# Strassen once more inside two of seven products: the second layer of a fused convolution and feed-forward kernel laid out by column tiles

## The chip, the cores and the metric

The kernel runs on one core of one Trainium2 chip. The metric is device time in microseconds (us) of that core. The profile comes from one execution recorded by the hardware profiler. Engines: TensorE (PE) multiplies, VectorE (DVE) and ScalarE (ACT) work elementwise on SBUF and PSUM, GpSimd (POOL) works elementwise on SBUF, SyncE (SP) issues most DMAs. Each runs its own queue in order, and semaphores make one wait for another.

## The reference

`x` is 8 x 4096 x 192, i.e. 32768 tokens of 192 features. A causal depthwise convolution of 7 taps (softmax of a weight per head) is followed by a feed-forward block with 2048 hidden units:

```python
out = np.einsum('hk,bskhg->bshg', w, x_unf)      # 7 taps, w = softmax(weight)
h = x @ w_in                                     # 192 -> 2048
g = h * np.clip(h + 3.0, 0.0, 6.0) / 6.0         # hard swish
return (g @ w_out).astype(np.float32)            # 2048 -> 192
```

All is fp32. The input arrives transposed, features ahead of tokens.

## The kernel before

**Rounds.** The tokens are cut into 32 blocks of 1024, each of two halves of 512 (index k). Round 0 is special (weights are still being loaded and prepared; `out_direct`, L364, does its second layer plainly). Rounds 1 to 31 (L775) are alike: `first_layer(i)` (L478), then `second_layer(i)` (L532). The schedule is written out by hand (`tc.manual_schedule`): the order of the calls in the source is each engine's order.

**First layer.** For each of 8 chunks c of hidden units and 2 groups (own and swapped halves) PE makes three accumulating passes (HIGH, LOW, MIX: the fp32 numbers are split into parts for the faster fp32r format) with row tiles of 64. ACT scales PSUM by 4097 between them (L501), then ACT (`relu`, L301) and DVE (`gate`, L305) make the activations `g`. Between groups DVE works through `jobs`: the taps of the next block's convolution (L729), and what is left over of the round before. [...]

**Second layer.** `g` is seen as a 2 x 2 block matrix A (token half by hidden half, each 8 chunks of 128), `w_out` as a 2 x 2 block matrix B (hidden half by output half of 96 columns). The product is done in the Strassen-Winograd form with seven products instead of eight:

```
S1 = A21+A22  S2 = S1-A11  S3 = A11-A21  S4 = A12-S2
T1 = B12-B11  T2 = B22-T1  T3 = B22-B12  T4 = T2-B21
P1 = A11 B11  P2 = A12 B21  P3 = S4 B22  P4 = A22 T4
P5 = S1 T1    P6 = S2 T2    P7 = S3 T3
```

Each product is 96 output columns, i.e. three thirds of 32 (index q, `QS` = 32), by 512 tokens, by 8 chunks. A matmul (`mm`, L336) has 32 columns and runs in one of four column tiles of PE (`tile_position`); `side_by_side` (L349) issues four streams in turn, so that four matmuls run together: a quartet. `three` (L420) puts a product's three thirds and a third of another into the four tiles, `four` (L413) any four parts, `by_quarters` (L423) cuts one third's chunks into four. Each quartet of streams fills one PSUM bank; ACT copies pieces out to SBUF (L437, L540), and DVE adds them up with the other banks (`add`, L445), transposes 32 x 32 blocks (`store`, L447) and hands the rows to SP to store. S3 is made by GpSimd (L401) pair by pair during the first layer, S1 by an accumulating DMA from GpSimd's queue (L528) but for the last pair, which DVE adds; S2 (into A11's place) and S4 (into A12's) by DVE (`g_sums`, L391) in the second layer. After the first layer `halves_of_y` (L751) splits the next block's convolution result and swaps its halves by DMA. `finish` (L566) is left for the next first layer, in the last round it is done in two halves of 256 tokens.

Of the kernel before, what the change touches and what calls it, by code (L numbers as in the profile page):

```python
# [8 lines left out]
ALU = mybir.AluOpType  # L9
# [16 lines left out]
def kernel(  # L26
# [34 lines left out]
    cst = ctx.enter_context(tc.tile_pool(name="cst", bufs=1))  # L61
    xs = ctx.enter_context(tc.tile_pool(name="xs", bufs=1))
    ys = ctx.enter_context(tc.tile_pool(name="ys", bufs=1))
    ot = ctx.enter_context(tc.tile_pool(name="ot", bufs=3))
    ps = ctx.enter_context(tc.tile_pool(name="ps", bufs=1, space=bass.MemoryType.PSUM))
    start_pools, first_in = ExitStack(), ExitStack()
    stg = start_pools.enter_context(tc.tile_pool(name="stg", bufs=8))
# [49 lines left out]
    w_out = cst.tile([P, NP, 7, DH], F32, name="w_out")  # L117
    B11, B12, B21, B22, T1, T2, T4 = range(7)
    T3 = B12

    w_in_bits = moe_w_in.bitcast(U32).rearrange("(p s) (c f w) -> c p s f w", s=K3, f=P, w=2)
    w_out_bits = moe_w_out.bitcast(U32).rearrange("(k c p) w -> p c k w", p=P, k=2)
# [230 lines left out]

    every = range(NP)

    def store_rows(i, k, q, xt, j, dma=nc.sync, tokens=slice(0, N)):

        t0 = i * TB + k * N
        dma.dma_start(
            out=out[t0 + tokens.start : t0 + tokens.stop, q * QS : (q + 1) * QS].rearrange("(t r) d -> r t d", r=QS),  # L360
            in_=xt[j * QS : (j + 1) * QS, tokens].rearrange("r (t d) -> r t d", d=QS),
        )

    def out_direct(i, work):  # L364

        parts = [(k, q) for k in range(G) for q in range(G * NQ)]
        for r in range(0, len(parts), 4):
            b = take()
            bank = psum[:, b]
            streams = []  # L370
            for j, (k, q) in enumerate(parts[r : r + 4]):
                streams.append([
                    m
                    for mms in zip(*(
                        mm(bank, j, dff_half(h * G + k), h * 2 + q // NQ, q % NQ, every,
                           h == 0, h == 1)
                        for h in range(2)
                    ))
                    for m in mms
                ])  # L380
            side_by_side(*streams)
            if r == 0:
                for u in work:
                    u()
            xt = ot.tile([P, N], F32, name="xt")
            nc.vector.transpose(out=xt[:], in_=bank)
            give(b)
            for j, (k, q) in enumerate(parts[r : r + 4]):
                store_rows(i, k, q, xt, j)

    def g_sums(engine, which, slots, width):  # L391

        forms = {
            3: (S3, A11, A21, ALU.subtract),
            2: (S2, S1, A11, ALU.subtract), 4: (S4, A12, S2, ALU.subtract),
        }
        for n in which:
            o, a, b, op = forms[n]
            for p in slots[::width]:
                r = slice(p, p + width)  # L400
                engine.tensor_tensor(out=o[:, r], in0=a[:, r], in1=b[:, r], op=op)  # L401


    prod = {
        1: (A11, B11), 2: (A12, B21), 3: (S4, B22), 4: (A22, T4),
        5: (S1, T1), 6: (S2, T2), 7: (None, T3),
    }

# [37 lines left out]

    def store(i, c, k, half_, qs=range(NQ), queues=(nc.sync,), tokens=slice(0, N)):  # L447

        xt = ot.tile([P, N], F32, name="xt")
        r = slice(qs[0] * QS, (qs[-1] + 1) * QS)  # L450
        nc.vector.transpose(out=xt[r, tokens], in_=c[r, tokens])  # L451
        for q in qs:
# [6 lines left out]
    def r32(ap):  # L459
        return ap.bitcast(F32R)  # L460
# [13 lines left out]
        nc.scalar.mul(r32(mix), mix, -4096.0)  # L474

    free_slots = list(range(4))

    def first_layer(i, jobs):  # L478

# [5 lines left out]
        def mms(n, part, start=False, stop=False):  # L485
            group, c = divmod(n, NP)
            for s in range(K3):
                for k in range(2):
                    r = slice(k * D2, (k + 1) * D2)
                    nc.tensor.matmul(  # L490
                        out=psum[:, 2 * slots[n] + k], lhsT=r32(w_in_parts[part][r, c, s]),
                        rhs=r32(y_parts[part][r, group, s]),
                        start=start and s == 0, stop=stop and s == K3 - 1,
                        skip_group_check=True,
                    )
# [20 lines left out]
        for n in range(count):  # L516
# [4 lines left out]
                begin(n + 2)  # L521
            for job in jobs.get(n, ()):
                job()
            if n > NP and n % 2:
                pair = slice(n - NP - 1, n - NP + 1)
                g_sums(nc.gpsimd, (3,), range(NP)[pair], 2)
                if n + 1 < count:
                    nc.gpsimd.dma_start(out=S1[:, pair], in_=A22[:, pair], accum_op=ALU.add)  # L528
                else:
                    add(S1[:, pair], A21[:, pair], A22[:, pair])  # L530

    def second_layer(i, between):  # L532
        last = i + 1 == NB
        ours = [free_slots.pop(0) for _ in range(3 + last)]
        free_banks[:] = [2 * n + k for n in ours for k in range(2)]
        both = nc.sync, nc.scalar
        p1, p2, p4, u2, u3 = (cs.tile([DH, N], F32, name=f"c{k}") for k in range(5))
        two, third = rows_of(0, 2), rows_of(2, 3)
        b, bank = three(1, 2, 0)
        nc.scalar.copy(out=p1[:], in_=bank[m])  # L540
        piece(p2, 0, bank, NQ)
        b, bank = four((2, 1), (2, 2), (4, 0), (4, 1))
        for dst, q, j in ((p2, 1, 0), (p2, 2, 1), (p4, 0, 2), (p4, 1, 3)):
            piece(dst, q, bank, j)
        g_sums(nc.vector, (2,), every, 4)
        add(p2[:], p1[:], p2[:])
        store(i, p2, 0, 0)
        p5 = cs.tile([DH, N], F32, name="c1")
        b7, bank7 = three(7, 4, 2)
        piece(p4, 2, bank7, NQ)  # L550
        g_sums(nc.vector, (4,), every, 4)
        b, bank = three(6, 5, 0)
        piece(p5, 0, bank, NQ)
        add(u2[:], p1[:], bank[m])
        add(u3[:], u2[:], bank7[m])
        add(p4[:], u3[:], p4[:], ALU.subtract)
        store(i, p4, 1, 0)
        for job in between:
            job()
        b, bank = by_quarters(5, 1)  # L560
        pieces(p5, 1, bank)
        add(u2[two], u2[two], p5[two])
        add(p5[two], u3[two], p5[two])
        store(i, p5, 1, 1, range(2))

        def finish(bank, **part):  # L566
            t = part.get("tokens", slice(0, N))
            add(u2[:, t], u2[:, t], bank[m, t])
            add(u2[third, t], u2[third, t], bank[rows(NQ), t])
            store(i, u2, 0, 1, **part)  # L570
            add(u3[third, t], u3[third, t], bank[rows(NQ), t])
            store(i, u3, 1, 1, range(2, 3), **part)

        if last:
            for t in range(0, N, N // 2):
                bank = psum[:, take()]
                ts = slice(t, t + N // 2)
                side_by_side(*[
                    product(bank, j, n, q, tokens=ts)
                    for j, (n, q) in enumerate([(3, 0), (3, 1), (3, 2), (5, 2)])  # L580
                ])
                finish(bank, queues=both, tokens=ts)
            return []
        b, bank = three(3, 5, 2)
        free_slots.extend(ours)
        return [lambda: finish(bank)]

    def rows_of(q0, q1):
        return slice(q0 * QS, q1 * QS)
# [18 lines left out]
    with tc.manual_schedule():  # L608
# [106 lines left out]
        while n < len(units):  # L715
# [1 line left out]
            clamp(n + 1)  # L717
            split(n + 2)
            n += 1
        w_sums(((T1, B12, B11), (T2, B22, T1), (T4, T2, B21)))  # L720
        start_pools.close()
        late = ctx.enter_context(tc.tile_pool(name="late", bufs=1, reuse_waits="tile"))
        w_in_parts = [late.tile([P, NP, K3, P], F32, name=f"w_in{n}") for n in range(3)]
# [8 lines left out]
                ))  # L732
            return jobs

        y_parts = []

        def y_high():
            high_of(y_parts[HIGH][:, 0], y[:])
            swap(y_parts[HIGH][:, 1], y_parts[HIGH][:, 0])

        def y_low():
            nc.vector.tensor_tensor(  # L742
                out=r32(y_parts[LOW][:, 0]), in0=y[:], in1=y_parts[HIGH][:, 0], op=ALU.subtract
            )
            swap(y_parts[LOW][:, 1], y_parts[LOW][:, 0])

        def y_mix():
            from_high(y_parts[MIX][:, 0], y_parts[HIGH][:, 0], 1.0 + EPS, y[:], ALU.subtract)
            swap(y_parts[MIX][:, 1], y_parts[MIX][:, 0])

        def halves_of_y():  # L751
            y_high()
            y_low()
            y_mix()

        def prepare():
            for n in range(0, NP, 4):
# [3 lines left out]
                job()  # L761
            first_in.close()
            later = ctx.enter_context(tc.tile_pool(name="later", bufs=1, reuse_waits="tile"))
            y_parts.extend(later.tile([P, 2, K3, N], F32, name=f"y{n}") for n in range(3))
            halves_of_y()
            x_tiles[2] = load_x(2, nc.gpsimd)

        out_direct(0, [prepare])
        w_sums(((T3, B22, B12),))
        last = ctx.enter_context(tc.tile_pool(name="last", bufs=1, reuse_waits="tile"))  # L770
        S3 = last.tile([P, NP, N], F32, name="s3")[:]
        cs = ctx.enter_context(tc.tile_pool(name="cs", bufs=1, reuse_waits="tile"))
        conv = conv_jobs(2)
        left = []
        for i in range(1, NB):  # L775
            jobs = {2 * n + 1: [job] for n, job in enumerate(conv[1:])}
            jobs[-1] = left
            if i == 1:
                jobs = {n + 2: job for n, job in jobs.items()}
                jobs[1] = conv[:1]  # L780
            first_layer(i, jobs)
            if i + 1 < NB:
                halves_of_y()
            if i + 2 < NB:
                x_tiles[i + 2] = load_x(i + 2)
            conv = conv_jobs(i + 2) if i + 2 < NB else []
            left = second_layer(i, conv[:1])


# [31 lines left out]
```

## Time and profile before

2251.72 us, the median of three runs (2251.39 to 2251.75).

| in the profile | us | share of the span |
|---|---|---|
| span | 2251.7 | |
| PE busy | 2242.8 | 100% |
| DVE busy | 1755.1 | 78% |
| ACT busy | 1313.6 | 58% |
| GpSimd busy | 493.9 | 22% |
| one second layer, from the chain in time | 36.19 | 31 of them |
| one first layer, from the chain in time | 32.98 | 31 of them |

The granted clock of TensorE is 0.999 of full speed. In the groups, one row is a source line with its engine, what it writes from what, how often, the busy time, the mean duration in ns, and how long its engine stood idle just before with what ended that. An fp32 matmul appears as two records, hence 336 in a second layer of 168 matmuls. The two stretches of a round from 1102.25 us on:

| stretch | PE | DVE | ACT | GpSimd | DMA share |
|---|---|---|---|---|---|
| second layer, 36.18 us | 36.18 | 25.02 | 10.06 | 7.20 | 0.67 |
| first layer, 32.98 us | 32.98 | 29.18 | 30.50 | 7.70 | 0.16 |

### The profile page before, as it was taken

What the parts mean: (1) busy time and instruction counts of PE and PEld (TensorE: products, weight loads), DVE (VectorE), ACT (ScalarE), POOL (GpSimd) and SP (SyncE); (2) the same over time, 40 slices, a digit from 0 to 9 for tenths busy, and PEclk for the clock granted to TensorE, in tenths of its full rate; (3) what the DMA queues carried; (4) which work ended last, traced back from release to release, by engine and by line L of the source; (5) the groups of instructions that cost most, each with busy time, mean ns of one, the idle gap of its engine ahead of it and who ended that gap; (6) DMA issues with size and microseconds to landing.
All of it is one profiled execution on the core that took longest, in us unless ns stands there. A gap on an engine that the chain in (4) does not pass through costs nothing.

```text
span 2251.7 us, 46078 instructions
## 1 busy us (share of the span) xinstructions
PE 2242.8 (100%) x20008; PEld 1213.1 (54%) x20008; DVE 1755.1 (78%) x1575; ACT 1313.6 (58%) x1428; POOL 493.9 (22%) x247
## 2 busy tenths in 40 slices
PE   9999999999999999999999999999999999999998
PEld 5445554455544555544555445555455554455544
DVE  8788787778877787877878777887778787787865
ACT  7456654466644666545666446664456654466643
POOL 2322201222112222022221122210222202222112
PEclk9999999999999999999999999999999999999999
DMA  6344335443345443354423554334544335443342
GB/s 155 71 93 90 53 64 99 96 92 63 58 90 99 89 82 53 75 99 92 95 53 59 99 99 89 66 57 87 99 91 85 54 69 99 95 94 56 61 79 43
DMA packets 262442, 182.55 MB, mean 81 GB/s; under 512 B 208992, under 2 KB 214112, under 8 KB 262240
## 3 DMA queue, kind: packets, MB, share of 16 engines
q1 hardware_dynamic: 235928, 129.59, 28.9%
q0 software_dynamic: 25616, 49.82, 12.7%
q8 instruction: 156, 2.56, 0.5%
q14 instruction: 46, 0.38, 0.1%
q10 hardware_dynamic: 696, 0.20, 0.0%
HBM read 31.72 MB, written 25.17 MB: 25 GB/s over the span
## 4 chain that ended last, share of the span: by engine, by line
PE 98%; DVE 1%; ACT 0%; DMA 0%; issue 0%; SPq 0%; ACTq 0%; DVEq 0%
PE psum L340 51%; PE psum L490 45%; PE psum L295 2%; DVE c L445 0%; DMA x<-in_x_dram 0%; DVE xt L451 0%; DVE y L729 0%; DMA out_dram<-xt 0%; ACT y L727 0%; ACT g L301 0%; SPq L100 0%; SPq L132 0%; DVE g L305 0%; DVE top L174 0%; PE psum L623 0%
## 5 line engine op out<-in xcount | busy, mean ns | idle before, releaser
L340 PE MATMUL psum<-g,w_out 128*32 128x512 f32 (+1 forms) x9376 | 1165.4, 590 | 0.0
L490 PE MATMUL psum<-y,w_in 64*128 64x512 f32 x8928 | 1025.1, 388 | 0.5 <-ACT psum L501 0.4
L490 PEld LDWEIGHTS psum<-y,w_in 64*128 64x128 f32 x8928 | 830.0, 184 | 207.9 <-issue 26.0
L401 POOL TENSOR_TENSOR s<-g 128x1024 f32<-128x1024 f32 x124 | 377.4, 3043 | 1624.1 <-DVE g L305 1623.2
L305 DVE SCALAR_TENSOR_TENSOR g<-g,psum 128x1024 f32<-128x1024 f32 (+1 forms) x528 | 618.6, 1186 | 129.8 <-ACT g L301 129.4
L340 PEld LDWEIGHTS psum<-g,w_out 128*32 128x32 f32 x9376 | 340.5, 110 | 650.4 <-issue 638.5
L501 ACT ACTIVATE psum<-psum 128x1024 f32<-128x1024 f32 x496 | 500.3, 1009 | 259.6 <-PE psum L490 257.6
L301 ACT ACTIVATE g<-psum,half 128x1024 f32<-128x1024 f32 (+1 forms) x528 | 565.0, 1088 | 0.8
L437 ACT COPY c<-psum 32x512 f32<-32x512 f32 x248 | 143.4, 578 | 516.4 <-PE psum L340 513.9
L729 DVE SCALAR_TENSOR_TENSOR y<-x,c_sb,y 128x1536 f32<-128x1536 f32 x186 | 337.0, 1812 | 0.2
L445 DVE TENSOR_TENSOR c<-c,psum 96x512 f32<-96x512 f32 (+2 forms) x251 | 170.7, 680 | 211.5 <-ACT c L437 183.2
L401 DVE TENSOR_TENSOR g<-g 128x2048 f32<-128x2048 f32 x124 | 276.8, 2272 | 0.0
L340 PE MATMUL psum<-s,w_out 128*32 128x512 f32 x1488 | 218.3, 592 | 0.0
L340 PEld LDWEIGHTS psum<-s,w_out 128*32 128x32 f32 x1488 | 61.2, 110 | 148.3 <-issue 148.3
L445 DVE TENSOR_TENSOR g<-g 128x1024 f32<-128x1024 f32 x31 | 38.0, 1226 | 130.7 <-POOL s L401 130.7
L528 POOL DMA_DIRECT2D g<-g x93 | 111.7, 1201 | 29.5 <-POOL s L401 29.5
L451 DVE STREAM_TRANSPOSE xt<-c 96x512 f32<-96x512 f32 (+4 forms) x157 | 109.7, 699 | 5.4
L445 DVE TENSOR_TENSOR c<-c,c 96x512 f32<-96x512 f32 (+1 forms) x124 | 84.8, 684 | 5.1 <-ACT c L437 1.9
L540 ACT COPY c<-psum 96x512 f32<-96x512 f32 x31 | 18.0, 581 | 115.7 <-PE psum L340 115.7
L742 DVE TENSOR_TENSOR y<-y,y 128x1536 fp32r<-128x1536 f32 x31 | 54.3, 1752 | 1.6 <-ACT y L463 1.6
L466 DVE SCALAR_TENSOR_TENSOR y<-y,y 128x1536 fp32r<-128x1536 f32 x31 | 54.3, 1752 | 0.0
L463 ACT ACTIVATE y<-y 128x1536 fp32r<-128x1536 f32 x31 | 46.6, 1503 | 12.4 <-DVE y L729 12.4
(53 smaller groups left out, 275.8 us busy)
## 6 DMA issues: line engine op xcount, KB each, us to landing
y<-y SPq DMA_DIRECT2D x186, 384.0 KB, 5.1
g<-g POOLq DMA_DIRECT2D x93, 512.0 KB, 5.3
out_dram<-xt SPq DMA_DIRECT2D x380, 64.0 KB, 2.0
x<-in_x_dram SPq DMA_DIRECT2D x53, 388.5 KB, 7.5
stage<-in_moe_w_in_dram SPq DMA_DIRECT2D x16, 192.0 KB, 4.6
stage<-in_moe_w_out_dram SPq DMA_DIRECT2D x8, 384.0 KB, 5.0
x<-in_x_dram SPq DMA_DIRECT2D x7, 384.0 KB, 7.4
x<-in_x_dram POOLq DMA_DIRECT2D x2, 388.5 KB, 5.5
```

Of the source, the lines that this page charges most:

```text
L301: nc.scalar.activation(r6, h, ACT.Relu, bias=half[:], scale=1.0 / 6.0)
L305: nc.vector.scalar_tensor_tensor(out=g_, in0=g_, scalar=1.0, in1=h, op0=ALU.min, op1=ALU.mult)
L340: lambda p=p: nc.tensor.matmul(out=bank[j * QS : (j + 1) * QS, tokens], lhsT=w_out[:, p, w, cols], rhs=x[:, p, tokens], start=(first and p ...
L401: engine.tensor_tensor(out=o[:, r], in0=a[:, r], in1=b[:, r], op=op)
L437: nc.scalar.copy(out=dst[rows(q)], in_=src[rows(j)])
L445: nc.vector.tensor_tensor(out=out, in0=x, in1=y, op=op)
L451: nc.vector.transpose(out=xt[r, tokens], in_=c[r, tokens])
L466: nc.vector.scalar_tensor_tensor(out=r32(out), in0=high, scalar=scale, in1=x, op0=ALU.mult, op1=op)
L490: nc.tensor.matmul(out=psum[:, 2 * slots[n] + k], lhsT=r32(w_in_parts[part][r, c, s]), rhs=r32(y_parts[part][r, group, s]), start=start an ...
L501: nc.scalar.mul(both(n), both(n), 4097.0)
L528: nc.gpsimd.dma_start(out=S1[:, pair], in_=A22[:, pair], accum_op=ALU.add)
L729: jobs.append(lambda k=k: nc.vector.scalar_tensor_tensor(out=y[:], in0=x[:, :, k : k + N], scalar=c_sb[:, k : k + 1], in1=y[:], op0=ALU.mu ...
```

## The change

Two of the seven products, P1 and P5, are computed for their first two thirds by the same seven-product form once more: 64 columns by 512 tokens by 8 chunks are split into 2 x 2 blocks of 32 columns, 256 tokens and 4 chunks (even and odd ones). Sixteen matmuls of 512 tokens become seven small products of four matmuls of 256 tokens. This needs small sums of A11 for P1 (made by GpSimd in the first layer, into a new tile `s1`), of S1 for P5 (made by DVE into A22's place once P4 has read it), and small sums of the weights (`w_s`, once).

The second layer is laid out anew around that. Column tiles 0 to 2 each take one third of P4, P7, P2, P6, P3; tile 3 takes all that is small, and the last thirds of P1 and P5. The last third of P1 is spread: one chunk in each of tiles 0, 1, 2, the others in tile 3, handed from tile to tile by an ACT copy from one row group of PSUM to another, onto which the next tile accumulates. In the same way products are added in PSUM: ACT writes P1 into bank `b`, P6 is accumulated onto it, DVE reads the sum, P3 is accumulated onto that. Six banks have fixed roles: `d` P4 (and small bank C), `e` the relay (and A), `b` P1 + P6 + P3 (and V), `x_` B, `a` P2 (and E), `c` P7. Each stream keeps a `clock` in units of half a matmul; all matmuls, copies and sums are sorted by it, and that is the order of issue.

Also moved: the y split and the swaps go from ahead of the second layer into it; S4 goes into S3's tile; the last S3 sum and one more S1 sum go to DVE; `xt` and the partial results share a tile in turn with `s1`; T4's sign is turned.

```diff
-    ot = ctx.enter_context(tc.tile_pool(name="ot", bufs=3))
+    ot = ctx.enter_context(tc.tile_pool(name="ot", bufs=1))
+    w_s = cst.tile([P, 2, 4, NP // 2, QS], F32, name="w_s")
...
-            2: (S2, S1, A11, ALU.subtract), 4: (S4, A12, S2, ALU.subtract),
+            2: (S2, S1, A11, ALU.subtract), 4: (S3, A12, S2, ALU.subtract),
...
+            if n < NP and n % 2:
+                small_sums(s1[-1], A11, (1, 2, 3, 4), nc.gpsimd, every[n - 1 : n + 1])
             if n > NP and n % 2:
-                g_sums(nc.gpsimd, (3,), range(NP)[pair], 2)
-                if n + 1 < count:
+                g_sums(nc.gpsimd if n + 1 < count else nc.vector, (3,), range(NP)[pair], 2)
+                if n + 3 < count:
                     nc.gpsimd.dma_start(out=S1[:, pair], in_=A22[:, pair], accum_op=ALU.add)
-                else:
-                    add(S1[:, pair], A21[:, pair], A22[:, pair])
+        for pair in (slice(NP - 2, NP), slice(NP - 4, NP - 2)):
+            add(S1[:, pair], A21[:, pair], A22[:, pair])
...
-        b, bank = three(1, 2, 0)
-        nc.scalar.copy(out=p1[:], in_=bank[m])
-        piece(p2, 0, bank, NQ)
-        b, bank = four((2, 1), (2, 2), (4, 0), (4, 1))
...
+        for q in range(NQ):
+            plain(q, d, 4, q, every, True)
+            before = (1, 6, NP)[q]
+            plain(q, c, 7, q, every[:before], True)
+            plain(q, e, 1, 2, range(5 + q, 6 + q))
+            do(clock[q], copy, out=e[rows(q + 1)] if q < 2 else p1[third], in_=e[rows(q)])
+            plain(q, c, 7, q, every[before:])
+            plain(q, a, 2, q, every[:6], True)
+            plain(q, b, 6, q, every)
+            plain(q, a, 2, q, every[6:])
+            plain(q, b, 3, q, every)
...
+            steps = {
+                1: lambda: copy(out=B[:, lo], in_=A[:, lo]),
+                2: lambda: copy(out=p()[first, lo], in_=A[:, lo]),
+                6: lambda: copy(out=C[:, lo], in_=B[:, lo]),
+                5: lambda: copy(out=p()[second, lo], in_=E[:, lo]),
+                7: lambda: add(p()[second, hi], C[:, lo], p()[second, lo]),
+                3: lambda: add(p()[second, lo], B[:, lo], p()[second, lo]),
+                4: lambda: copy(out=p()[first, hi], in_=C[:, lo]),
+            }
+            to = {1: A, 2: A, 6: B, 5: E, 7: C, 3: B, 4: C}
...
+        level_two(1, lambda: p1, range(5), "1 x5 6 5 2 7 3 4")
+        do(14, copy, out=e[first], in_=V)
+        level_two(5, lambda: late["p5"], range(NP), "1 x2 2 6 5 7 3 x1 4 x5")
+        for t, job in between:
+            do(t, job)
+        for t, n in ((16.2, 1), (16.2, 2), (30.5, 3), (34.5, 4)):
+            do(t, small_sums, s5, S1, (n,), nc.vector)
+        do(32, tiles)
+        do(34, lambda: copy(out=late["p7"], in_=c[m]))
+        do(38, copy, out=b[m], in_=p1[:])
+        do(38, g_sums, nc.vector, (2,), every, 4)
+        do(38, g_sums, nc.vector, (4,), every, 4)
+        do(62, lambda: add(late["u3"], b[m], late["p7"]))
+        do(62, lambda: add(late["p7"], late["u3"], d[m]))
...
+        do(82, lambda: copy(out=late["p5"][third], in_=V))
+        events = sorted(((t, fn) for st in streams for t, fn in st), key=lambda x: x[0])
...
-                halves_of_y()
+                between = [(13, split_high), (15, split_rest), (18, swap_parts)]
             if i + 2 < NB:
-                x_tiles[i + 2] = load_x(i + 2)
+                between += [(20, begin_conv), (60, lambda: conv[0]())]
```

Here `plain` queues full matmuls of one third (cost 2 on its tile's clock), `small` a small product of four half-width ones (cost 1 each), `x5` in an order means five plain chunks of the last third, and `do(t, ...)` puts other engines' work just ahead of clock t.

## The prediction, made before the changed kernel was run

> **What bounds the kernel now.** I read the busy shares first, then the chain that ended last, then the same chain in order of time, then the groups.
>
> ```profile
> PE 2242.8 (100%) x20008; PEld 1213.1 (54%) x20008; DVE 1755.1 (78%) x1575; ACT 1313.6 (58%) x1428; POOL 493.9 (22%) x247
> PE 98%; DVE 1%; ACT 0%; DMA 0%; issue 0%; SPq 0%; ACTq 0%; DVEq 0%
> ```
>
> TensorE (PE) is busy all through and makes 98% of the chain. A busy PE may still be a slow one, so look at the chain in time, one round of the main loop (start, length, what):
>
> ```profile
> 1102.25 36.19 PE psum L340 x336
> 1138.43 32.98 PE psum L490 x288
> ```
>
> A second layer (L340) takes 36.19 us, a first layer (L490) 32.98, and 31 such rounds follow each other with the same lengths: no gap is left to close, only matmuls to leave out. The weight loads of TensorE by time give its rate, and the last round holds the one sample of 256-wide tiles:
>
> ```profile
> 1102.63 0.13 PEld L340 LDWEIGHTS psum<-g,w_out 128*32 128x32 f32 x4 [0.30 <-issue]
> 1103.06 0.13 PEld L340 LDWEIGHTS psum<-g,w_out 128*32 128x32 f32 x4 [0.30 <-issue]
> ...
> 2238.03 6.61 PEld L340 LDWEIGHTS psum<-g,w_out 128*32 128x32 f32 x124 [0.30 <-issue]
> ```
>
> The groups give the price of everything else (busy us, mean ns):
>
> ```profile
> L305 DVE SCALAR_TENSOR_TENSOR g<-g,psum 128x1024 f32<-128x1024 f32 x496 | 598.3, 1218 | 128.0 <-ACT g L301 127.9
> L401 POOL TENSOR_TENSOR s<-g 128x1024 f32<-128x1024 f32 x124 | 377.4, 3043 | 1624.1 <-DVE g L305 1623.2
> L729 DVE SCALAR_TENSOR_TENSOR y<-x,c_sb,y 128x1536 f32<-128x1536 f32 x186 | 337.0, 1812 | 0.2
> L401 DVE TENSOR_TENSOR g<-g 128x2048 f32<-128x2048 f32 x124 | 276.8, 2272 | 0.0
> L437 ACT COPY c<-psum 32x512 f32<-32x512 f32 x248 | 143.4, 578 | 516.4 <-PE psum L340 513.9
> L445 DVE TENSOR_TENSOR c<-c,psum 96x512 f32<-96x512 f32 x92 | 62.9, 684 | 206.2 <-ACT c L437 183.2 <-PE psum L340 22.0
> L445 DVE TENSOR_TENSOR g<-g 128x1024 f32<-128x1024 f32 x31 | 38.0, 1226 | 130.7 <-POOL s L401 130.7
> L340 PE MATMUL psum<-g,w_out 128*32 128x256 f32 x128 | 7.1, 379 | 0.0
> ```
>
> **The rate.** Four column tiles start together every 0.43 us (1102.63, 1103.06), two such passes to one fp32 matmul: 0.86 us for a quartet of four matmuls, and 36.19 / 42 = 0.862. At half width (last weight-load row): 124 loads are 31 passes; less the 0.13 of the last, 6.48 us over 30 steps are 0.216 a pass, 0.432 a matmul, half of the full one within 1%. Loads of 110 ns stay hidden there, so twice the instructions per us do not bind.
>
> [...] if a half-width matmul held its place until the wide ones beside it end, it would cost a full step. [...] Here all tiles are of one width at any moment, so the trace doesn't decide; but every fp32 matmul is two passes, and the first passes of all four tiles come before the second of any (8 loads, then 4 per 0.43 us), though the kernel issues whole matmuls one tile after another. That looks like independent tiles, and I take it so. [...]
>
> **The change, part by part.**
>
> *Matmuls.* Before: 7 products x 3 thirds x 8 chunks = 168 = 42 quartets. After, tiles 0 to 2 each run P4, P7, P2, P6, P3 (5 x 8) and one chunk of P1's last third: 41. Tile 3 runs the other 5 chunks of that third and 8 of P5's (13), and twice seven small products of 4 matmuls of 256 tokens: 56 halves = 28. Again 41, so all tiles end together: 41 x 0.862 = 35.33, **0.86 us less** a round. The halves cost 0.432 against 0.431 of this average, or 0.4294 if 0.8588 is the inner step: up to 56 x 0.0026 = 0.15. I take 35.46, 0.73 less.
>
> *Vector work.* Per round DVE gains one 128x1024 sum S3 (from GpSimd), one S1 sum, and four 128x(4x256) small sums, 1.23 each: +7.4. The combining of products before is some 12 adds and 5 transposes at about 0.69 (11.7); after, 5 adds and 4 transposes (6.2) and four 32x256 adds at 0.43 (the row of that shape in the last round), 1.7. Net +3.6 on 54.2 us of 69.2 (the two stretches of one round: 25.0 in the second layer, 29.2 in the first). It still fits, so only moments count. DVE in the first layer is unchanged (16 gates, 6 taps: 30 of 33 us; the left-over stores 2.8 against 3.5).
>
> *GpSimd.* 16 sums of 128x256 in the first layer; at the 128x1024 row's rate 0.76 each = 12.2 us, less one sum and one DMA issue (4.2): 15 becomes 23 us of 69. Ready long before the second layer. It could slow DVE through a shared path, but the taps last 1806 to 1821 ns with GpSimd running or not; it is GpSimd that stretches (2.39 to 3.93). Cost 0.
>
> *ACT.* Relay copies of 32x512 and 32x256 replace eight pieces: about level. The y split moves some 2 us later and its swaps by 7 us; they are needed halfway through the next first layer, over 30 us on. Cost 0. Small weight sums: 8 of 128x128 on GpSimd once, before any use. Cost 0.
>
> *New waits, all in front of PE, whose queue blocks for all tiles.* Times from the second layer's start, unit 0.43 (half a matmul). From PE's last pass to a reader is 0.28 (first product ends at 7.17 - 0.28, its copy starts 1109.35).
> 1. P1's last third goes from tile 0 to 1 to 2 through an ACT copy in PSUM. The second hop: tile 1 ends at unit 30 = 12.9, copy 13.15 to 13.65 or 13.75 (0.58, or 0.5 if PSUM to PSUM is as much cheaper as L501 is than L301), tile 2 wants it at unit 32 = 13.75, its weights 0.1 before. **Stall 0 to 0.15.** The first hop has 3.4 us.
> 2. P1's small product 4 waits for the DVE add that reads product 7. DVE in its order, at the pitch of the timeline (1.14 per 1024, 1.67 per 1536, 2.2 per 2048): gates to 3.5, S3 and two S1 sums 6.9, y split 10.3, two small sums 12.6; add 13.2 to 13.65. Due at unit 34 = 14.6. Margin 0.9.
> 3. P6 waits for S2: small sums 3 and 4 and one add to 16.6, first half of S2 to 18.9, due at unit 46 = 19.8. Margin 0.9; the second half 21.1 against 23.2.
> 4. P3 adds onto the bank that DVE must first read (u3). S4 ends at 25.5; small 7 of P5 ends at unit 62 = 26.7, add 27.0 to 27.45, u3 to 28.15, due at unit 66 = 28.35. **Margin 0.2**, the thinnest for DVE.
>
> I take 0.1 a round for 1 and 4 together. Saved per round 0.73 - 0.1 = 0.63; over 31 rounds 19.5.
>
> *Ends.* The last round had its final adds half hidden by 256-wide matmuls; now after PE's end there are a copy (0.28 + 0.58) and four adds and four transposes of 96x256 (0.42, 0.44): about 4.3, then 2.65 to the landing: 7.0 against 6.6. +0.4. The first 100 us are alike.
>
> 2251.7 - 19.5 + 0.4 = **2232.6 us**.
>
> **Rivals.**
> - *No stall at all.* Both thin handoffs hold: 31 x 0.73 = 22.6, 2229.5; with the halves' surcharge gone too, 26.7 and 2225.4. For it: the margins are computed positive. Against: hop 1 has none.
> - *Handoffs eat the gain.* The small sums with a step of two chunks, or copies beside PE in the same bank, run slower, and 1 to 4 cost 0.4 to 0.7 a round: 31 x 0.33 down to 31 x 0.03 is left, 2242 to 2251. For it: four handoffs within 15 us on one blocking queue. Against: PE waits on DVE for 9.0 us in all today.
> - *Slower: DVE or tiles bind.* If DVE comes 1.2 us late at 2 and again at 4, the stall is 0.3 plus 1.0, over 0.73 by 0.57: 2252 + 31 x 0.57 = 2270. If a half-width matmul held a full step: 56 x 0.43 = 24 more a round, near 2970. For it: DVE waits for PE twice in the middle, and a late PE makes DVE late again. Against: the two-pass order above.
>
> **How the numbers follow.** Forecast 0.55, no stall 0.18, handoffs eat the gain 0.13, slower 0.14. The no-change band (2247.2 to 2256.2) takes about half of the third and a little of the others: faster 0.79, same 0.07, slower 0.14. Range 2226 to 2250: it leaves out the slower case and the ends of the second and third.
>
> **What would show it.** Second layers in the chain of 35.4 to 35.7 us with first layers still 32.98 confirm the count; a round's length is the sum. Idle PE weight loads waiting on ACT near 13.7 us or DVE near 28.3 us into the second layer show steps 1 and 4; waits near 14.6 or 19.8 that DVE's order is longer than I worked out. I am wrong if the 256-wide rows in the timeline are not 0.43 apart beside 512-wide ones, if first layers lengthen (GpSimd or DVE late there), or if DVE's small sums last well over 1.3 us.

## The result and the profile after

The changed kernel takes 2268.9 us (median, against 2251.7 before): **slower** by 0.8%, a ratio of 1.0077 (95% interval 1.0064 to 1.009). 2232.6 was forecast. Times here are medians of the executions at a granted clock of 0.999 or 1.0; one of the four of the last experiment's kernel (`e7_two_taps_moved`) took 4597.8 us at a clock of 0.964 and is left out. The span in the profile grows from 2251.7 to 2266.7 us. The busy shares and the chain of the page of after:

```profile
PE 2252.5 (99%) x21432; PEld 1517.4 (67%) x21432; DVE 1909.8 (84%) x1636; ACT 1389.4 (61%) x1676; POOL 914.2 (40%) x689
PE 65%; DVE 22%; ACT 5%; issue 2%; ACTq 0%; DVEq 0%
```

PE still looks busy (99%), but its share of the chain falls from 98% to 65%: for a fifth of the time it is DVE that sets the pace. The chain of after in order of time, one round (start, length, what), says where:

```profile
1147.02 2.97 PE psum L510 x24
...
1155.33 1.81 DVE y L861
1157.14 2.31 DVE g L306 x2
1159.45 2.13 DVE y L861
1161.58 2.27 DVE g L306 x2
...
1176.05 5.10 PE psum L510 x42
1181.15 35.47 PE psum L609 x216
```

The second layer (L609) is one unbroken piece of 35.47 us, where it was 36.19. That is the gain that was meant, 0.72 a round. The first layer (1147.02 to 1181.15, 34.1 us, where it was 32.98) is no longer one piece: the chain runs through DVE's taps (L861) and gates (L306), pair after pair, 4.43 us each, where PE needs 4.1. Net 0.4 a round lost: from the end of round 1's second layer to PE's end before took 2075.0 us, after 2086.7.

The groups of after, by shape, show which instruction of DVE has changed:

```profile
L306 DVE SCALAR_TENSOR_TENSOR g<-g,psum 128x1024 f32<-128x1024 f32 x496 | 585.6, 1212 | 130.9 <-ACT g L302 130.8
L861 DVE SCALAR_TENSOR_TENSOR y<-x,c_sb,y 128x1536 f32<-128x1536 f32 x186 | 388.0, 2086 | 0.2
L573 POOL TENSOR_TENSOR s<-g 128x256 f32<-128x256 f32 x248 | 359.8, 1451 | 1211.5 <-DVE g L306 1202.3 <-DMA out_dram<-results 9.2
```

The gate is as fast as before (1218, now 1212). The tap, the same instruction on the same data, takes 2086 ns on average instead of 1812. No wait is shown for it: idle before it is 0.2 us in all. The loss hides *inside the duration*. DVE and GpSimd in time, in one stretch of after:

```profile
1157.06 2.39 DVE L306 SCALAR_TENSOR_TENSOR g<-g,psum 128x1024 f32<-128x1024 f32 x2
1159.37 2.21 DVE L861 SCALAR_TENSOR_TENSOR y<-x,c_sb,y 128x1536 f32<-128x1536 f32 x1
```

```profile
1158.52 0.75 POOL L573 TENSOR_TENSOR s<-g 128x256 f32<-128x256 f32 x1
1159.21 0.75 POOL L573 TENSOR_TENSOR s<-g,s 128x256 f32<-128x256 f32 x1
1159.92 2.26 POOL L573 TENSOR_TENSOR s<-g 128x256 f32<-128x256 f32 x1
```

The tap at 1159.37 begins while a GpSimd sum (1159.21 to 1159.96) runs, and is 0.4 us longer than its 1.81. The next GpSimd sum begins at 1159.92, and is 1.5 longer than its 0.74: it ends 0.6 after the tap. This reads as if each waits, once, for the instruction of the other that is running. The gates beside the middle sums are not held up: the two from 1157.06 on take 2.39 us, and 2.43 at 1148.47 in before, where no GpSimd sum runs.

### The profile page after: what moved, and what is told of

The parts are those of the page before. It is cut to its first block, busy times and chain, and to the rows that moved or that the text cites. A ratio compares the mean times of both kernels' runs of the same rounds, so it can differ in the third digit from the quotient of the medians.

```text
span 2266.7 us, 50172 instructions
## 1 busy us (share of the span) xinstructions
PE 2252.5 (99%) x21432; PEld 1517.4 (67%) x21432; DVE 1909.8 (84%) x1636; ACT 1389.4 (61%) x1676; POOL 914.2 (40%) x689
## 4 chain that ended last, share of the span: by engine, by line
PE 65%; DVE 22%; ACT 5%; issue 2%; ACTq 0%; DVEq 0%
PE psum L609 48%; PE psum L510 17%; DVE y L861 11%; DVE g L306 11%; ACT g L302 3%; ACT psum L521 2%; DVE y L479 0%; DVE y L877 0%; DVE results L458 0%; DVE g L573 0%; DVE results L464 0%; ACTq L521 0%; ACT results L709 0%; DVE p L458 0%; DVEq L464 0%
## 5 line engine op out<-in xcount | busy, mean ns | idle before, releaser
L609 PE MATMUL psum<-g,w_out 128*32 128x512 f32 (+1 forms) x6696 | 968.3, 553 | 0.0
L573 POOL TENSOR_TENSOR s<-g 128x256 f32<-128x256 f32 x248 | 359.8, 1451 | 1211.5 <-DVE g L306 1202.3
L306 DVE SCALAR_TENSOR_TENSOR g<-g,psum 128x1024 f32<-128x1024 f32 (+1 forms) x528 | 605.9, 1180 | 132.7 <-ACT g L302 132.4
L510 PE MATMUL psum<-y_other,w_in 64*128 64x512 f32 x4464 | 548.3, 394 | 4.4 <-DVE g L306 0.7
L609 PEld LDWEIGHTS psum<-g,w_out 128*32 128x32 f32 x6696 | 367.8, 110 | 249.0 <-issue 127.2
L510 PE MATMUL psum<-y,w_in 64*128 64x512 f32 x4464 | 522.1, 388 | 0.6 <-ACT psum L521 0.4
L510 PEld LDWEIGHTS psum<-y_other,w_in 64*128 64x128 f32 x4464 | 406.8, 184 | 135.9 <-DVE g L306 50.6
L510 PEld LDWEIGHTS psum<-y,w_in 64*128 64x128 f32 x4464 | 413.5, 184 | 117.2 <-issue 26.0
L609 PE MATMUL psum<-s,w_out 128*32 128x512 f32 (+1 forms) x3224 | 465.3, 576 | 0.0
L861 DVE SCALAR_TENSOR_TENSOR y<-x,c_sb,y 128x1536 f32<-128x1536 f32 x186 | 388.0, 2086 | 0.2
L609 PE MATMUL psum<-g,w_s 128*32 128x256 f32 x1240 | 282.8, 379 | 0.2 <-DVE p L458 0.2
L609 PEld LDWEIGHTS psum<-s,w_out 128*32 128x32 f32 x3224 | 151.7, 110 | 82.7 <-issue 50.8
L414 DVE TENSOR_TENSOR s<-g 128x2048 f32<-128x2048 f32 (+1 forms) x93 | 187.0, 2038 | 1.1
L609 PEld LDWEIGHTS psum<-g,w_s 128*32 128x32 f32 x1240 | 136.3, 110 | 69.4 <-DVE p L458 1.1
L609 PE MATMUL psum<-s,w_s 128*32 128x256 f32 x744 | 170.7, 379 | 0.0
```

Source lines behind the costliest of these rows:

```text
L306: nc.vector.scalar_tensor_tensor(out=g_, in0=g_, scalar=1.0, in1=h, op0=ALU.min, op1=ALU.mult)
L510: nc.tensor.matmul(out=psum[:, 2 * slots[n] + k], lhsT=r32(w_in_parts[part][r, c, s]), rhs=r32(y_other[0][r, part, s] if group else y_own[ ...
L573: engine.tensor_tensor(out=o, in0=p, in1=q, op=op)
L609: nc.tensor.matmul(out=out, lhsT=w, rhs=x, start=start, stop=True, tile_position=(0, j * QS), skip_group_check=True,)
L861: jobs.append(lambda k=k: nc.vector.scalar_tensor_tensor(out=y[:], in0=x[:, :, k : k + N], scalar=c_sb[:, k : k + 1], in1=y[:], op0=ALU.mu ...
```

## The experiments

These are the explanations that the runs were to tell apart. **Theory 1.** A tap reads two tensors in SBUF (x and y), and so does a GpSimd sum; of two such instructions the one that starts second is held up, and a GpSimd instruction that reads nothing holds no tap up. The four small sums of each pair of chunks collide with the next tap, and DVE, with 29.2 of 33 us filled in the first layer, can't make up for it. **Theory 2.** The moved y split and swaps, or DVE's new order, make the first layer late. **Rival 1b.** Any GpSimd work on SBUF would hold DVE up.

**Without the small sums** (`e1_no_small_sums`):

```diff
-            if n == 1:
-                s1.append(ot.tile([P, NP, N], F32, name="s1", tag="shared")[:])
-            if n < NP and n % 2:
-                small_sums(s1[-1], A11, (1, 2, 3, 4), nc.gpsimd, every[n - 1 : n + 1])
...
-            sums, ws = (s1[-1], w_s[:, 0]) if n == 1 else (s5, w_s[:, 1])
+            sums, ws = (A11, w_s[:, 0]) if n == 1 else (s5, w_s[:, 1])
```

> The changed kernel without the 16 small sums of GpSimd in the first layer: P1's small products read A11's blocks in their place, so P1's values are left out of the comparison, and everything else stands. Theory 1 (GpSimd's small sums hold up DVE's taps[...]): taps back from 2086 ns mean to 1812, first layers back from 34.2 to 33.0 us, second layers still 35.47, rounds of 68.45; the span falls by some 31 x 1.1 + 2 for the first round, to 2231 us, ratio to before 0.991. Theory 2 (the moved y split and swaps, or the new order of DVE, make the first layer late): unchanged, 2267 us.

Measured 2232.2 us, ratio 0.9914 (0.9899 to 0.9929), span 2231.3. The taps in its groups:

```profile
L857 DVE SCALAR_TENSOR_TENSOR y<-x,c_sb,y 128x1536 f32<-128x1536 f32 x186 | 339.3, 1824 | 0.2
```

and two second layers in its chain, 68.42 us apart:

```profile
204.18 35.47 PE psum L605 x216
272.60 35.47 PE psum L605 x216
```

All of the loss goes with the sums. Theory 2 falls: split, swaps and order stand as in the changed kernel.

**GpSimd as busy, but only writing** (`e2_write_only`):

```diff
-                small_sums(s1[-1], A11, (1, 2, 3, 4), nc.gpsimd, every[n - 1 : n + 1])
+                for _ in range(4):
+                    nc.gpsimd.memset(s1[-1][:, n - 1 : n + 1], 0.0)
```

> The changed kernel with each GpSimd small sum replaced by a memset of 128x1024 into the same tile: GpSimd is as busy at the same moments and writes SBUF, but reads nothing (P1's small sums are zeros). Theory 1: [...] taps of 1812 ns, first layers 33.0, span 2231 us. Rival 1b (any work of GpSimd on SBUF holds DVE up): taps of over 2000 ns and a span near 2267 us. Theory 2: 2267 us with taps of 2086.

Measured 2232.1 us, ratio 0.9912 (0.9896 to 0.9929), span 2230.6. GpSimd's writes in one first layer, and the taps in the groups:

```profile
1067.13 15.82 POOL L548 MEMSET s<- 128x1024 f32 x16 [38.44 <-DMA out_dram<-results]
```

```profile
L862 DVE SCALAR_TENSOR_TENSOR y<-x,c_sb,y 128x1536 f32<-128x1536 f32 x186 | 337.4, 1814 | 0.2
```

The writes do not come at the moments of the sums, as I had expected: they read nothing, so they wait for no gate, and all 16 run back to back. They still serve, for they fill 15.8 us of a first layer, more than the sums without their waits (16 at some 0.74, 11.8 us). In this round four taps, begun at 1068.71, 1072.74, 1076.82 and 1080.90, lie wholly beside them, and each takes 1.81 us. Rival 1b falls: writing alone does not hold a tap up, and what a sum does beyond it is to read and add.

**The sums alone, in the kernel before** (`e3_sums_in_before`), into a spare tile:

```diff
...
+            if n < NP and n % 2:
+                small_sums(spare[0], A11, (1, 2, 3, 4), nc.gpsimd, every[n - 1 : n + 1])
             if n > NP and n % 2:
...
+        spare.append(last.tile([P, 2, N], F32, name="spare")[:])
```

> The kernel before with the 16 GpSimd small sums added after chunks 1, 3, 5, 7 of the first layer, into a spare tile that nobody reads; nothing else of the change. Theory 1: taps stretch to about 2090 ns and first layers grow by 1.1 us as in the changed kernel: 2252 + 31 x 1.1 = 2286 us, ratio 1.015. Theory 2: nothing waits for these sums, so 2252 us.

Measured 2288.4 us, ratio 1.0163 (1.0147 to 1.0178). Its taps and its second layers:

```profile
L746 DVE SCALAR_TENSOR_TENSOR y<-x,c_sb,y 128x1536 f32<-128x1536 f32 x186 | 388.1, 2086 | 0.2
```

```profile
205.24 36.19 PE psum L340 x336
275.61 36.19 PE psum L340 x336
```

2086 ns to the digit of the changed kernel; rounds of 70.37 instead of 69.17. Nothing waits for these sums' results and the second layers keep their 36.19, so what is lost is lost beside the sums in the first layer: 36.6 us in all against runs of before taken alongside (2251.8), or 1.2 a round.

**Three sums per pair, the fourth in one piece at the seam** (`e4_three_then_one`), an attempt to keep all the work and have none of the loss:

```diff
-                small_sums(s1[-1], A11, (1, 2, 3, 4), nc.gpsimd, every[n - 1 : n + 1])
+                small_sums(s1[-1], A11, (1, 2, 3), nc.gpsimd, every[n - 1 : n + 1])
...
                     nc.gpsimd.dma_start(out=S1[:, pair], in_=A22[:, pair], accum_op=ALU.add)
+                if n == 11:
+                    small_sums(s1[-1], A11, (4,))
```

> The changed kernel with the fourth small sum of every pair (x12 - s2) moved: three sums per pair stay after chunks 1, 3, 5, 7, and the fourth is done for all eight chunks in one instruction of 128x1024 after GpSimd's last DMA issue at chunk 11, when no tap is left. Nothing is left out. Theory 1: after a tap of 1.81 us the gap until the next is about 2.3 us (two gates); four sums of 0.72 need 2.9 and run into the next tap by 0.45, three need 2.2 and do not: taps 1812 to 1850 ns, first layers 33.0, span 2231 to 2234 us, faster than both kernels. [...] Theory 2: 2267 us.

Measured 2273.4 us, ratio 1.0096 (1.0081 to 1.0111): a miss, and slower than the changed kernel. The stretches of one round, first and second layer (start and end, length, then the busy us of PE, its weight loads, DVE, ACT and GpSimd with their instructions, and last the clock, the DMA share and GB/s):

```profile
1149.10:1182.08 32.98, 32.98 (x296) 26.79 (x294) 28.34 (x23) 31.00 (x32) 22.41 (x15) 1.00 0.16 26
1182.08:1218.90 36.82, 36.50 (x388) 18.69 (x386) 31.60 (x25) 12.02 (x21) 5.97 (x3) 1.00 0.57 115
```

The first layer is healed, 32.98, as expected. The second is now 36.82 instead of 35.47. GpSimd and DVE at its start:

```profile
1183.01 2.87 POOL L575 TENSOR_TENSOR s<-g,s 128x1024 f32<-128x1024 f32 x1
1185.38 2.83 POOL L414 TENSOR_TENSOR s<-g 128x1024 f32<-128x1024 f32 x1
```

```profile
1185.67 3.62 DVE L414 TENSOR_TENSOR s<-g 128x1024 f32<-128x1024 f32 x1
```

I had taken GpSimd to be free before the seam, the border of the two layers. Its queue was not: the wide sum began only 0.9 us into the second layer and ended 3.8 us into it, with the regular S3 sum behind. DVE's own S3 sum, which also reads two tensors in SBUF, stands behind that: 3.62 us where it took 1.43 in the changed kernel. DVE comes some 2 us late to the handoffs, and its margin of 0.9 is spent:

```profile
PEld psum L611 <- DVE p L458: 36.5, 29, 1.8
PEld psum L611 <- DVE g L414: 21.7, 30, 0.7
```

These are the handoffs 2 and 3 of the prediction. The wait behind a wide instruction was a long one here: 2.2 us more than in the changed kernel.

**Three sums, the fourth left out** (`e8_three_sums`; the third stands in for it), to tell the seam from the first layer:

```diff
-                small_sums(s1[-1], A11, (1, 2, 3, 4), nc.gpsimd, every[n - 1 : n + 1])
+                small_sums(s1[-1], A11, (1, 2, 3), nc.gpsimd, every[n - 1 : n + 1])
...
+            if n == 1:
+                z4 = z3
```

> As the run with three small sums per pair, but the fourth sum (x12 - s2) is left out altogether (the third stands in for it), so that nothing wide is added on GpSimd at the layers' seam. Theory 1: the loss of that run came only from the wide fourth sum, behind which DVE's S3 sum waited (3.6 us instead of 1.4), so here first layers 33.0, second layers 35.47 and a span of 2231 us. If three sums per pair still cost something in the first layer: between 2235 and 2255 us.

Measured 2234.0 us, ratio 0.9922 (0.9905 to 0.9938), second layers of 35.47 every 68.43 us. Three sums per pair cost nothing to be seen (taps of 1830 ns); the miss of the run before was the seam.

**Two taps moved** (`e7_two_taps_moved`), with all the work done:

```diff
             jobs = {2 * n + 1: [job] for n, job in enumerate(conv[1:])}
+            if i > 1:
+                jobs = dict(zip((1, 5, 9, 11), ([job] for job in conv[3:])))
...
                 between += [(20, begin_conv), (60, lambda: conv[0]())]
+                between += [(76, lambda: conv[1]()), (78, lambda: conv[2]())]
```

> The changed kernel with two of the six DVE taps of a round moved out of the first layer to the end of the second layer, where DVE stands idle 4.7 us waiting for ACT's last copy, and the other four placed behind chunks 1, 5, 9 and 11, so that between two taps GpSimd has time for its four small sums. All the work is done. Theory 1 (a tap and a GpSimd sum wait for each other's end, at most one instruction each time; only the coincidence costs): taps of 1810 to 1830 ns, first layers 33.0, second layers 35.47, rounds 68.45; the first round keeps its six taps, so span 2231 to 2234 us, ratio 0.991 to 0.992, faster than both kernels. If DVE's total of work in a round were what binds, nothing is gained: 2267 us. If the moved taps delay what follows at the start of the next first layer: first layers over 33.3 and 2240 to 2250 us.

Measured 2233.7 us, ratio 0.9921 (0.9904 to 0.9938): **faster than both kernels**, by 18.0 us than before and by 35.2 than the change as it was. The taps in its groups, and in one round the last of eight GpSimd sums with the tap that follows:

```profile
L861 DVE SCALAR_TENSOR_TENSOR y<-x,c_sb,y 128x1536 f32<-128x1536 f32 x186 | 338.0, 1817 | 1.2
```

```profile
1144.96 0.75 POOL L573 TENSOR_TENSOR s<-g,s 128x256 f32<-128x256 f32 x1
1146.27 1.81 DVE L861 SCALAR_TENSOR_TENSOR y<-x,c_sb,y 128x1536 f32<-128x1536 f32 x1
```

Same taps, same sums, the same engines; only the moments differ. With a tap at every second pair of chunks, the eight sums of two pairs are done (1145.71) before the next tap starts. Second layers are 35.47 and rounds 68.40 in its chain. That DVE's total of work binds is ruled out with it.

## Why the prediction was wrong, point by point

- **The count of matmuls and their rate: right.** 35.46 us was forecast for a second layer, 35.47 measured. The weight loads of after show it: in each step of 0.43 us the three wide tiles load once, and the fourth, with 256-wide matmuls, twice.

```profile
1187.54 0.12 PEld L609 LDWEIGHTS psum<-s,w_out 128*32 128x32 f32 x3
1187.57 0.33 PEld L609 LDWEIGHTS psum<-s,w_s 128*32 128x32 f32 x2
```

  So a tile is not held by its wider neighbours here: a narrow matmul did not cost a full step, which by the prediction's estimate would have been 24 us more a round.
- **The four handoffs: right but for round 1, with more room than I gave them.** PE's weight loads wait 13.8 us in all for the relay copy, 0.2 each, and the piece stays unbroken; the 0.1 a round that I charged is not there. The three 32x512 copies a round from PSUM to PSUM take 549 to 553 ns each, within the 0.5 to 0.58 us that I took.
- **"Cost 0" for GpSimd: the step that failed.** I wrote that GpSimd "could slow DVE through a shared path, but the taps last 1806 to 1821 ns with GpSimd running or not". That was true, and no evidence. This is one round of before, a tap, the GpSimd sum beside it and the next tap:

```profile
1163.06 1.81 DVE L729 SCALAR_TENSOR_TENSOR y<-x,c_sb,y 128x1536 f32<-128x1536 f32 x1
1163.22 3.92 POOL L401 TENSOR_TENSOR s<-g 128x1024 f32<-128x1024 f32 x1 [53.34 <-DVE g L305]
1167.14 1.81 DVE L729 SCALAR_TENSOR_TENSOR y<-x,c_sb,y 128x1536 f32<-128x1536 f32 x1
```

  The sum was released by the gate that stands just before the tap, and began 0.16 us after it: it was GpSimd that stood behind (3.92 us where 2.39 is its shortest), and it was over as the next tap began. A tap that began while a sum ran did not occur before, so its price could not be read off; but the stretched sum, which I had noted, was itself the sign that one of the two waits. The runs give the rest: the taps take 2086 ns on average in the runs with four sums a pair and 1814 with writes in their place; the gates, with one input in PSUM, take 1212 ns in after and 1218 before; and before, where the tap came first, the sum waited (3.92 us), while after, where the sum came first, the tap did (2.21 us). What inside the chip makes them wait is not shown: the runs show only who waits beside what.
- **The sum that would have shown it.** In a pair of chunks PE takes 4.1 us. In the trace of after an unhindered tap holds DVE for 1.73 (1155.33 to the gate at 1157.06), and sums start 0.70 apart (1158.52, 1159.21, 1159.92). If a tap and a sum never run side by side, a tap and four sums need 1.73 + 4 x 0.70 = 4.5, an estimate from these starts; the pair measured 4.43. With three sums it is 3.8, which fits, and that run lost nothing. I added up each engine's own time, and never the time of the taps and the sums together. The term set to 0 measured 1.1 us a first layer; against the 0.72 gained, that turns the sign.
- **Of the rivals**, the slower one had the right side but not the cause: it looked for DVE's lateness in the second layer. What I had put under "what would show it" (first layers lengthen, GpSimd or DVE late there) is what came.
- The rest of the 15 us: by the end of its second layer round 1 is 2.4 us later than before. Its taps collide too (up to 2.38 us), and in its second layer DVE's S3 sum, behind a GpSimd sum, took 3.49 us, so that the add for handoff 2 came late and PE's loads waited 1.1: from 150.56 to 151.63 us no weights are loaded for any tile, though only tile 3's product needed the add. The tail costs 0.9 instead of 0.4.

## What to carry to other kernels

When work goes to an idle engine, add up not only that engine's time but the time of those of its instructions and of the busy one's that hold each other up: here DVE's taps and GpSimd's sums, both with two inputs in SBUF (taps of 2086 ns beside the sums, 1812 before), per stretch between two deadlines. A duration that is steady beside a neighbour may show only that it came first (1.81 us for the tap, 3.92 for the sum beside it); look at who started first before you read it as "no contention". Such a wait showed here as a longer instruction, not as idle time (0.2 us before 186 taps), so compare mean durations of unchanged instructions first; and keep what can stand in front of a critical engine narrow, or at another moment.

## What I had not expected of the hardware

In the round of after shown above, taps and GpSimd sums take turns. The tap at 1159.37 loses 0.4 us, less than the 0.59 that the running sum of 0.75 still has to go by the trace; the next sum does not come ahead of it but takes 2.26 us instead of 0.74. So what DVE lost, here and at the seam of `e4_three_then_one`, was at most one instruction of the other side: 0.4 us behind 128x256, and 2.4 us behind 128x1024 (3.62 where DVE's other sums of that shape, L575 in that run, take 1.22). That it is 0.4 again and again, at four of the six taps of the round shown, goes with a lock step: in after, pair upon pair, both engines' queues repeat with the same 4.43 us. Where the tap begins with no sum running, as the first of a round (1.81), it loses nothing.
